# A six-layer cross network on one core: the second layer's weights on another DMA queue, and small loads moved to GpSimd's queue

## The chip, the cores and the metric

The kernel runs on one NeuronCore of a Trainium2 chip. The metric is the device time of one execution in microseconds (us), the median of several runs. Engine names in the profile: PE is TensorE (PEld its weight loads), DVE is VectorE, ACT is ScalarE, POOL is GpSimd, and SP is SyncE, which here only issues DMAs. "SPq" and "ACTq" are DMAs issued by SP and by ACT.

## The reference

```python
B, F, D, L = 4096, 26, 16, 6
Din = min(F * D, 1024)                 # 416
# x0: (4096, 416)   ws: (6, 416, 416)   bs: (6, 416), all bfloat16
def reference(x0, ws, bs):
    x = x0
    for l in range(ws.shape[0]):
        x = x0 * (x @ ws[l] + bs[l]) + x
    return x
```

Layer l needs all 416 features of layer l-1, so the six layers are strictly one after the other for each row; the 4096 rows are independent.

## The kernel before, in words

**Tiling.** The rows are cut into four blocks (`s`, 1024 rows), each into two halves (`h`, 512 rows). The data is kept with features on partitions: 416 = 3 x 128 main features (chunks `c`, `m` or `k`, `DF` = 384) and a tail of 32 (`DR`). The tail of the four quarters of a block sits on the four groups of 32 partitions. The kernel keeps sums in PSUM over the layers: layer l adds its product onto what is there, and VectorE makes the next input from it in one instruction per chunk and half, (PSUM + summed bias) x x0 (`leave`, line 429). ScalarE, GpSimd and two small copies do the same for the tail (`leave_tail` with `tail_halves`, line 439, the product in line 452, and `swap`, lines 416 and 418).

**One layer on TensorE**, in this order: `main` for half 0 (36 matmuls), `tail_rows` (the tail features as inputs; weights `wt_sb` and, for tail to tail, `wc_sb`), `tail_outs` (the tail as output, 12 matmuls over both halves), `main` for half 1 (36 matmuls). Nearly all matmuls are recorded under line 285, the helper `mm`.

**Weights.** `w_sb[:, l]` holds rows 0 to 383 of layer l ("W0" comes in three pieces, "W1" to "W5" each in one DMA of 312 KB by `load_main`). `wt_sb[:, l]` holds the 32 tail rows, four copies, one for each group of partitions ("wt0" is layer 0, "wt1" layer 1, "wt2" layers 2 to 5). `wc_sb` is zero but for the 32x32 corner of each layer (tail rows, tail columns), placed at four positions. In the kernel before, GpSimd zeroes `wc_sb` (line 272) and copies each corner out of `wt_sb` (`corner`, line 278): layer 0 ahead of the loop, layer 1 after the tail of layer 0, layers 2 to 5 after the tail of layer 1.

**Head.** The first 512 rows of x0 come in plainly (`xin_sb`, half by SP, half by ACT), are transposed on TensorE (line 500) and copied out of PSUM by VectorE and, for chunk 1, by ScalarE (lines 510 and 515). The other 512 rows of block 0 come by one transposing DMA (`load_transposed`, line 205) and their tail columns plainly (`xtl_sb`); `tail_in` brings the tail of block 0 into place through TensorE and one ScalarE copy (line 405) to `x0t_sb`. `bias_sums` needs the bias vectors in `bsa_sb[1:7]`, a row of ones and a small triangular matrix `u_sb`; ScalarE copies the sums to `cb_sb` (line 534).

**Order.** Every engine works through its instructions in the order in which they are added. `Plan.add` (line 28) derives the waits from the keys an operation reads and writes; operations on one engine do not wait for each other, except where a result is read (GpSimd's operations that shift data between partitions wait for the ones they depend on). DMAs of one queue are issued in program order. SP issues x0's first rows, W0, `xtl`, the transposing load, then W1, wt1, W2, wt2, W3 to W5, and the later blocks of x0; ACT issues x0's second rows, the bias vectors, wt0.

Of the kernel before, what the change touches and what calls it, by code (L numbers as in the profile page):

```python
# [15 lines left out]
class Plan:  # L16
# [11 lines left out]
    def add(self, eng, fn, reads=(), writes=(), adds=(), parts=(), dma=None, shifts=False):  # L28
        if eng == "gpsimd" and dma is None:
            if shifts:  # L30
                adds = tuple(adds) + (("shift",),)
            else:
                reads = tuple(reads) + (("shift",),)
        op = Op()
        op.eng, op.fn, op.marked, op.dma, op.waits = eng, fn, False, dma, []
        needs = []
        for key in tuple(reads) + tuple(adds):
            needs += [(w, True) for w in self.writer.get(key, ())]
            if key[0] == "ps":
                needs += [(r, False) for r in self.readers.get(key, ())]  # L40
        for key in tuple(writes) + tuple(adds):
            needs += [(w, True) for w in self.writer.get(key, ())]
            needs += [(r, False) for r in self.readers.get(key, ())]
        for key in parts:
            needs += [(r, False) for r in self.readers.get(key, ())]
        clock = self.clock[eng]
        for need, raw in sorted(needs, key=lambda n: -n[0].idx):
            lane = need.group if need.dma else need.eng
            if dma and need.dma == dma:
                continue  # L50
            if need.dma is None and need.eng == eng and dma is None and (eng == "tensor" or not raw):
                continue
            if clock.get(lane, -1) >= need.idx:
                continue
            op.waits.append(need)
            need.marked = True
            for lane2, idx in need.clock.items():
                clock[lane2] = max(clock.get(lane2, -1), idx)
            clock[lane] = max(clock.get(lane, -1), need.idx)
        op.idx = len(self.ops[eng])  # L60
        op.group = None
        if dma:
            op.group = ("dma", dma)
            members = self.groups.setdefault(op.group, [])
            members.append(op)
            op.marked = True
        op.clock = dict(clock)
        self.ops[eng].append(op)
        for key in reads:
            self.readers.setdefault(key, []).append(op)  # L70
        for key in parts:
            if self.readers.get(key):
                self.writer[key], self.readers[key] = [], []
            self.writer.setdefault(key, []).append(op)
        for key in tuple(writes) + tuple(adds):
            old = self.writer.get(key, ())
            keep = [w for w in old if dma and w.dma == dma]
            self.writer[key] = keep + [op]
            if not keep:
                self.readers[key] = []  # L80
        return op
# [37 lines left out]
def bass_standalone__dcn_v2_cross__recsys_kernel(  # L119
# [22 lines left out]
    with ExitStack() as es:  # L142
# [45 lines left out]
        def load(queue, dst, src, name, writes):  # L188
            P.add(queue, lambda e: e.dma_start(dst, src), writes=writes, dma=name)  # L189

        def load_main(l):
            load(
                "sync", w_sb[:, l, :, :], ws[l, 0:DF, :].rearrange("(k p) n -> p k n", p=128), "w%d" % l, [("w", l)]
            )

        def load_rows(queue, i):
# [33 lines left out]
        load_rows("scalar", 1)  # L230
        for k in CH:
            load("sync", w_sb[:, 0, k, :], ws[0, 128 * k:128 * k + 128, :], "w0_%d" % k, [("w", 0, k)])
        load("scalar", bsa_sb[1:L + 1, :], bs[:, :], "bs", [("bs",)])
        load(
            "scalar", wt_sb[:, 0, :], ws[0, DF:D, :].unsqueeze(0).to_broadcast([4, DR, D]), "wt0", [("wt", "wt0")]
        )
        load("sync", xtl_sb[:, 4:JS, :], x0_v[:, 4:JS, DF:D], "xtl0", [("xtl", 0)])
        load_transposed(0, H, SB)
        load_main(1)
        load_tail_weights(1, 2, "wt1")  # L240
        load_main(2)
        load_tail_weights(2, L, "wt2")
# [3 lines left out]
        for s in range(1, NS):  # L246
# [16 lines left out]
            ), reads=[("ones",)], writes=[("ident",)],  # L263
        )
        P.add("gpsimd", lambda e: e.memset(bsa_sb[0:1, :], 1.0), writes=[("bs1",)])
        P.add(
            "gpsimd", lambda e: e.affine_select(
                out=u_sb[:, :], in_=ones_sb[0:L + 1, 0:L], pattern=[[1, L]],
                compare_op=ALU.is_ge, fill=0.0, base=1, channel_multiplier=-1,
            ), reads=[("ones",)], writes=[("u",)],  # L270
        )
        P.add("gpsimd", lambda e: e.memset(wc_sb[:, :, :, :], 0.0), writes=[("wc", "wt%d" % i) for i in range(3)])

        def corner(a, b, name):
            for g in range(4):
                p = quad(g | 1)
                P.add(
                    "gpsimd", lambda e, p=p, g=g: e.tensor_copy(  # L278
                        out=wc_sb[p, a:b, g % 2, quad(g)], in_=wt_sb[p, a:b, DF:D]
                    ), reads=[("wt", name), ("wc", name)], writes=[("wc", name, g)], shifts=True,  # L280
                )


# [47 lines left out]
        def tail_rows(s, l, start):  # L331
            src, key = src_tail(s, l)
            keys = [("wt", wkey(l)), key, key + ("swapped",)]

            def rows(pe, q, h, m, begin):
                for part in range(2):
                    if q % 2 == 0:
                        if part:
                            break
                        dst, rhs = ps[:, bank(h, m), :], src[quad(q), :, :]  # L340
                    else:
                        dst, rhs = ps[:, bank(h, m), part * G:(part + 1) * G], src[quad(q), 1 - part, :]
                    ins = mm(
                        pe, dst, wt_sb[quad(q), l, m * 128:(m + 1) * 128], rhs, begin and part == 0, (32 * q, 0)
                    )
                return ins

            def first(pe):
                for q in range(4):
                    h, m = divmod(q, 2)  # L350
                    ins = rows(pe, q, h, m, l == 0 and h == 1)
                return ins

            def second(pe):
                for q in range(4):
                    h = q // 2
                    if q % 2 == 0:
                        ins = rows(pe, q, h, 2, l == 0 and h == 1)
                    else:
                        for part in range(2):  # L360
                            ins = mm(
                                pe, ps[:, T_BANK[h], 0:G], wc_sb[quad(q), l, part, :], src[quad(q), 1 - part, :],
                                start and part == 0, (32 * q, 0),
                            )
                return ins

            P.add("tensor", first, reads=keys, adds=[("ps", bank(h, m)) for h in HALVES for m in range(2)])
            P.add(
                "tensor", second, reads=keys + [("wc", wkey(l), g) for g in range(4)],
                adds=[("ps", bank(h, 2)) for h in HALVES] + [("ps", T_BANK[h]) for h in HALVES],  # L370
            )

# [121 lines left out]
        for i in range(2):  # L494
            for c in CH:
                b = HEAD_BANKS[i][c]

                def fn(pe, i=i, c=c, b=b):
                    for j in range(2):
                        ins = pe.transpose(  # L500
                            out=psT[:, b, j * 128:(j + 1) * 128],
                            in_=xin_sb[:, 2 * i + j, c * 128:(c + 1) * 128], identity=ident[:, :],
                        )
                    return ins

                P.add("tensor", fn, reads=[("xin", i), ("ident",)], adds=[("ps", b)])
                dst, src = x0T_sb[:, c, i * 256:(i + 1) * 256], psT[:, b, 0:256]
                if c == 1:
                    P.add(
                        "scalar", lambda e, d=dst, s=src: e.activation(out=d, in_=s, func=ACTF.Copy),  # L510
                        reads=[("ps", b)], writes=[("x0Tp", c, i)],
                    )
                else:
                    P.add(
                        "vector", lambda e, d=dst, s=src: e.tensor_copy(out=d, in_=s),  # L515
                        reads=[("ps", b)], writes=[("x0Tp", c, i)],
                    )
# [20 lines left out]
            )  # L538


        corner(0, 1, "wt0")
        for s in range(NS):
            for l in range(L):
                ending = s == NS - 1 and l == L - 2
# [22 lines left out]
                leave_tail(s, l, not ending)  # L567
                if l == 2 and 0 < s < NS - 1:
                    place_tail(s + 1)
                if s == 0 and l == 0:  # L570
                    corner(1, 2, "wt1")
                if s == 0 and l == 1:
                    corner(2, L, "wt2")
                if l == 1 and s > 0:
                    store_block(s - 1)
                if ending:
# [151 lines left out]
```

## Time and profile before

| what | us |
|---|---|
| median of 3 runs (129.32 to 129.96) | 129.5 |
| the profiled execution, its own time | 130.31 |
| span of that execution on the core | 128.7 |
| TensorE busy | 124.5 (97% of the span) |
| VectorE busy | 98.3 |
| ScalarE busy | 44.3 |
| GpSimd busy | 39.6 |

The span is the part of an execution that the profile covers; 1.6 us of the profiled execution lie outside it. The granted TensorE clock is 1.0 over the span. A line of the timeline has the start, the duration (from the first to the last of a group), the engine, the line of the kernel, the operation, the tiles, the count, and in brackets how long the engine sat idle before it and what ended that.

### The profile page before, as it was taken

To read this page: it belongs to the slowest core of one execution; us is meant where nothing else is said; L and a number is where in the kernel's file an instruction comes from. 1 tells how busy PE (TensorE), PEld (TensorE's weight loads), DVE (VectorE), ACT (ScalarE), POOL (GpSimd) and SP (SyncE) were. 2 spreads that over 40 slices of the span, in tenths; PEclk is the share of its full clock that TensorE was granted. 3 is DMA by queue.
4 is the path that set the end of the run, shared out by engine and by line. 5 is a ranking of instruction groups with operands and counts; after the bars stand their busy time and mean duration, and the time that the engine had idled before them with its cause. 6 is when DMAs were issued, how large, how long until landed. Compare 5 with 4: busy or idle time off the path is not lost.

```text
span 128.7 us, 5290 instructions
## 1 busy us (share of the span) xinstructions
PE 124.5 (97%) x2402; PEld 64.5 (50%) x2402; DVE 98.3 (76%) x150; ACT 44.3 (34%) x97; POOL 39.6 (31%) x88
## 2 busy tenths in 40 slices
PE   7998999999999999999999999999999999999991
PEld 5553545545545545545545545545455455455660
DVE  0319489698797797797797797797797797797973
ACT  1525233343313243252222252252222252253920
POOL 7024273142122243242221251341320341440550
PEclk9999999999999999999999999999999999999999
DMA  3987999019999994500009407200008906100017
GB/s 110 198 203 184 265 210 231 21 37 233 195 177 240 172 166 157 156 8 5 0 5 189 81 0 248 63 5 0 0 5 167 103 5 216 54 0 5 0 38 232
DMA packets 34998, 14.11 MB, mean 110 GB/s; under 512 B 25690, under 2 KB 34976, under 8 KB 34976
## 3 DMA queue, kind: packets, MB, share of 16 engines
q1 hardware_dynamic: 34272, 13.24, 49.3%
q10 hardware_dynamic: 704, 0.54, 1.3%
q8 instruction: 19, 0.31, 1.0%
q14 instruction: 3, 0.02, 0.2%
HBM read 3.87 MB, written 3.41 MB: 57 GB/s over the span
## 4 chain that ended last, share of the span: by engine, by line
PE 88%; SPq 4%; DMA 4%; DVE 0%; issue 0%
PE ps L285 88%; DMA w_sb<-in_ws_dram 4%; SPq L205 2%; SPq L189 2%; DVE o_sb L659 0%
## 5 line engine op out<-in xcount | busy, mean ns | idle before, releaser
L429 DVE SCALAR_TENSOR_TENSOR xT_sb<-ps,cb_sb,x0T_sb 128x512 bf16<-128x512 f32 x120 | 80.9, 743 | 20.3 <-PE ps L285 20.3
L285 PE MATMUL ps<-xT_sb,w_sb 128*32 128x512 bf16 (+1 forms) x1596 | 84.2, 364 | 0.6 <-DMA w_sb<-in_ws_dram 0.6
L285 PEld LDWEIGHTS ps<-xT_sb,w_sb 128*32 128x32 bf16 x1596 | 40.8, 97 | 38.1 <-issue 4.0
L439 ACT ACTIVATE t_sb<-ps,cb_sb 64x256 f32<-64x256 f32 x46 | 21.6, 469 | 57.7 <-PE ps L285 57.4
L452 POOL TENSOR_TENSOR xt_sb<-t_sb,x0t_sb 128x256 bf16<-128x256 f32 x20 | 13.4, 672 | 63.4 <-ACT t_sb L439 63.4
L416 ACT ACTIVATE xt_sb<-xt_sb 32x256 bf16<-32x256 bf16 x38 | 15.7, 414 | 15.4 <-POOL xt_sb L452 15.2
L285 PE MATMUL ps<-x0T_sb,w_sb 128*32 128x512 bf16 (+1 forms) x336 | 19.3, 373 | 0.0
L418 POOL COPY xt_sb<-xt_sb 32x256 bf16<-32x256 bf16 x38 | 14.9, 392 | 2.4
L429 DVE SCALAR_TENSOR_TENSOR xo_sb<-ps,cb_sb,x0T_sb 128x512 bf16<-128x512 f32 x18 | 12.1, 744 | 2.5 <-PE ps L285 2.5
L285 PEld LDWEIGHTS ps<-x0T_sb,w_sb 128*32 128x32 bf16 x336 | 8.4, 98 | 7.6 <-issue 0.8
L285 PE MATMUL ps<-xt_sb,wt_sb 32*128 32x512 bf16 (+1 forms) x152 | 11.7, 326 | 0.0
L285 PE MATMUL ps<-xt_sb,wc_sb 32*128 32x256 bf16 x76 | 7.4, 268 | 0.0
L285 PEld LDWEIGHTS ps<-xt_sb,wt_sb 32*128 32x128 bf16 x152 | 2.4, 91 | 8.3 <-DVE xT_sb L429 6.4
L452 POOL TENSOR_TENSOR xot_sb<-t_sb,x0t_sb 128x256 bf16<-128x256 f32 x3 | 2.0, 672 | 9.9 <-ACT t_sb L439 9.9
L285 PE MATMUL ps<-w_sb,xT_sb 128*32 128x416 bf16 (+1 forms) x60 | 5.1, 339 | 0.0
L278 POOL COPY wc_sb<-wt_sb 32x32 bf16<-32x32 bf16 (+1 forms) x12 | 2.8, 233 | 5.1 <-DMA wt_sb<-in_ws_dram 4.5
L659 DVE TENSOR_TENSOR o_sb<-ps,xr_sb 128x416 bf16<-128x416 f32 x6 | 3.4, 587 | 1.3 <-PE ps L285 1.0
L293 PE MATMUL ps<-const-bfloat16-1.0 128*128 128x256 bf16 x14 | 3.1, 415 | 0.8 <-PEq L713 0.8
L285 PEld LDWEIGHTS ps<-xt_sb,wc_sb 32*128 32x128 bf16 x76 | 3.8, 93 | 0.2
L515 DVE COPY x0T_sb<-ps 128x256 bf16<-128x256 bf16 x4 | 1.1, 292 | 3.5 <-PE ps L500 3.2
L461 ACT ACTIVATE sS_sb<-ps,cb_sb 128x512 bf16<-128x512 f32 x5 | 3.0, 692 | 0.0
L285 PEld LDWEIGHTS ps<-w_sb,xT_sb 128*32 128x32 bf16 (+1 forms) x60 | 2.3, 97 | 1.4 <-issue 0.2
(39 smaller groups left out, 28.8 us busy)
## 6 DMA issues: line engine op xcount, KB each, us to landing
out_dram<-o_sb SPq DMA_DIRECT2D x3, 832.0 KB, 4.2
w_sb<-in_ws_dram SPq DMA_DIRECT2D x5, 312.0 KB, 4.4
xr_sb<-in_x_dram SPq DMA_DIRECT2D x1, 832.0 KB, 6.3
wt_sb<-in_ws_dram SPq DMA_DIRECT2D x4, 104.0 KB, 2.9
out_dram<-o_sb SPq DMA_DIRECT2D x2, 208.0 KB, 2.2
w_sb<-in_ws_dram SPq DMA_DIRECT2D x3, 104.0 KB, 3.6
xin_sb<-in_x_dram SPq DMA_DIRECT2D x1, 208.0 KB, 3.0
xin_sb<-in_x_dram ACTq DMA_DIRECT2D x1, 208.0 KB, 3.3
```

Source lines behind the costliest of these rows:

```text
L189: P.add(queue, lambda e: e.dma_start(dst, src), writes=writes, dma=name)
L205: "sync", lambda e: e.dma_start_transpose(x0T_sb[:, :, s * SB + a:s * SB + b], x0[s * SB + a:s * SB + b, 0:DF]),
L278: "gpsimd", lambda e, p=p, g=g: e.tensor_copy(out=wc_sb[p, a:b, g % 2, quad(g)], in_=wt_sb[p, a:b, DF:D]), reads=[("wt", name), ("wc", nam ...
L285: return pe.matmul(dst, lhsT=lhsT, rhs=rhs, start=start, stop=True, skip_group_check=True, tile_position=pos,)
L293: ins = pe.matmul(ps[:, 7, 0:256], lhsT=const[:, 0:128], rhs=const, start=True, stop=True)
L416: fn = lambda e, d=dst, s=src: e.activation(out=d, in_=s, func=ACTF.Copy)
L418: fn = lambda e, d=dst, s=src: e.tensor_copy(out=d, in_=s)
L429: "vector", lambda e: e.scalar_tensor_tensor(out=dst, in0=ps[:, bank(h, c), :], scalar=cb_sb[:, c, l:l + 1], in1=x0T_sb[:, c, o:o + H], op ...
L439: "scalar", lambda e, p=p, h=h: e.activation(out=dst[p, :], in_=ps[p, T_BANK[h], 0:G], func=ACTF.Identity, bias=cb_sb[p, NC, l:l + 1]), re ...
L452: "gpsimd", lambda e: e.tensor_tensor(out=dst, in0=t, in1=x0t_sb[:, s, 0, :], op=ALU.mult),
L461: fn = lambda e: e.activation(out=o, in_=i, func=ACTF.Identity, bias=b)
L659: "vector", lambda e: e.tensor_tensor(out=o_sb[:, jj, :], in0=ps[:, b, 0:D], in1=xr_sb[:, j, :], op=ALU.mult), reads=[("ps", b), ("xr",)], ...
```

## The change

W1 is issued by ACT, right behind wt0, and no longer by SP behind the transposing load. The bias vectors are issued by GpSimd's queue and no longer by ACT. The zeroing of `wc_sb` goes from GpSimd to VectorE. The corners of layers 1 to 5 are brought in by four DMAs on GpSimd's queue straight from `ws` (each 32 partitions x 5 layers x 64 bytes), right behind the build of `u_sb`; only layer 0's corner is still copied by GpSimd from `wt_sb`. Of the two PSUM copies of chunk 1 in the head, the first goes from ScalarE to VectorE. A GpSimd operation that shifts data waits for earlier GpSimd operations that do not shift.

```diff
@@ Plan.add
         for key in tuple(writes) + tuple(adds):
             needs += [(w, True) for w in self.writer.get(key, ())]
-            needs += [(r, False) for r in self.readers.get(key, ())]
+            needs += [(r, key == ("shift",)) for r in self.readers.get(key, ())]
@@ loads
-        def load_main(l):
+        def load_main(l, queue="sync"):
             load(
-                "sync", w_sb[:, l, :, :], ...
+                queue, w_sb[:, l, :, :], ...
             )
...
-        load("scalar", bsa_sb[1:L + 1, :], bs[:, :], "bs", [("bs",)])
         load(
             "scalar", wt_sb[:, 0, :], ws[0, DF:D, :].unsqueeze(0).to_broadcast([4, DR, D]), "wt0", [("wt", "wt0")]
         )
+        load_main(1, "scalar")
         load("sync", xtl_sb[:, 4:JS, :], x0_v[:, 4:JS, DF:D], "xtl0", [("xtl", 0)])
         load_transposed(0, H, SB)
-        load_main(1)
         load_tail_weights(1, 2, "wt1")
         load_main(2)
@@ GpSimd's start
         P.add("gpsimd", lambda e: e.memset(bsa_sb[0:1, :], 1.0), writes=[("bs1",)])
+        P.add("gpsimd", lambda e: e.dma_start(bsa_sb[1:L + 1, :], bs[:, :]), writes=[("bs",)], dma="bs")
...
-        P.add("gpsimd", lambda e: e.memset(wc_sb[:, :, :, :], 0.0), writes=[("wc", "wt%d" % i) for i in range(3)])
-
-        def corner(a, b, name):
+        P.add("vector", lambda e: e.memset(wc_sb[:, :, :, :], 0.0), writes=[("wc",)])
+        for g in range(4):
+            P.add(
+                "gpsimd", lambda e, g=g: e.dma_start(
+                    wc_sb[quad(g | 1), 1:L, g % 2, quad(g)], ws[1:L, DF:D, DF:D].rearrange("l p n -> p l n")
+                ), reads=[("wc",)], writes=[("wc1",)], dma="wc",
+            )
+
+        def corner():
             for g in range(4):
                 p = quad(g | 1)
                 P.add(
-                    "gpsimd", lambda e, p=p, g=g: e.tensor_copy(
-                        out=wc_sb[p, a:b, g % 2, quad(g)], in_=wt_sb[p, a:b, DF:D]
-                    ), reads=[("wt", name), ("wc", name)], writes=[("wc", name, g)], shifts=True,
+                    "gpsimd", lambda e, p=p, g=g: e.tensor_copy(out=wc_sb[p, 0, g % 2, quad(g)], in_=wt_sb[p, 0, DF:D]),
+                    reads=[("wt", "wt0"), ("wc",)], writes=[("wc0", g)], shifts=True,
                 )
@@ tail_rows
-                "tensor", second, reads=keys + [("wc", wkey(l), g) for g in range(4)],
+                "tensor", second, reads=keys + ([("wc1",)] if l else [("wc0", g) for g in range(4)]),
@@ head copies
-                if c == 1:
+                if i and c == 1:
                     P.add("scalar", ...)
@@ main loop
-        corner(0, 1, "wt0")
+        corner()
...
-                if s == 0 and l == 0:
-                    corner(1, 2, "wt1")
-                if s == 0 and l == 1:
-                    corner(2, L, "wt2")
```

More of the change, by code (lines that the diff above doesn't have):

```diff
@@ L189, in load @@
             P.add(queue, lambda e: e.dma_start(dst, src), writes=writes, dma=name)
-        def load_main(l):
+        def load_main(l, queue="sync"):
             load(
-                "sync", w_sb[:, l, :, :], ws[l, 0:DF, :].rearrange("(k p) n -> p k n", p=128), "w%d" % l, [("w", l)]
+                queue, w_sb[:, l, :, :], ws[l, 0:DF, :].rearrange("(k p) n -> p k n", p=128), "w%d" % l, [("w", l)]
             )
```

## Prediction

> **What bounds the kernel now.** I read the chain of work that ended last first, since it says which engine carries the end and what stands in front of it.
>
> ```profile
> 3.49 3.18 SPq L205 DMA_TRANSPOSE x0T_sb<-in_x_dram  x1
> 6.66 0.05 issue
> 6.71 5.47 DMA w_sb<-in_ws_dram
> 12.18 0.04 issue
> 12.22 113.84 PE ps L285 x2160
> ```
>
> From 12.22 us on TensorE carries the end alone. What releases it there is W1: issued by SP at 6.71, behind a transposing load whose issue holds SP for 3.18 us, it lands 5.47 us later. So a microsecond won before 12.22 is worth a microsecond, and so is any later hole in TensorE's row. The timeline of the first 30 us shows the holes.
>
> ```profile
> 7.01 1.00 POOL L278 COPY wc_sb<-wt_sb 32x32 bf16<-32x32 bf16 x4 [3.76 <-DMA wt_sb<-in_ws_dram]
> 7.27 0.10 PEld L285 LDWEIGHTS ps<-ident,xin_sb 128*32 128x32 bf16 x2
> 8.58 0.12 PEld L285 LDWEIGHTS ps<-x0t_sb,wt_sb 32*128 32x128 bf16 x8 [0.55 <-ACT x0t_sb L405]
> 8.71 0.21 PEld L285 LDWEIGHTS ps<-x0t_sb,wc_sb 32*128 32x128 bf16 x4
> 12.22 2.13 PE L285 MATMUL ps<-xT_sb,w_sb 128*32 128x512 bf16 x36 [0.64 <-DMA w_sb<-in_ws_dram]
> 14.28 0.12 PEld L285 LDWEIGHTS ps<-xt_sb,wt_sb 32*128 32x128 bf16 x8 [0.42 <-issue]
> 18.14 1.34 POOL L278 COPY wc_sb<-wt_sb 32x128 bf16<-32x128 bf16 x4
> 19.16 0.76 PE L285 MATMUL ps<-xt_sb,wt_sb 32*128 32x512 bf16 x7
> 24.19 0.60 PE L285 MATMUL ps<-xt_sb,wt_sb 32*128 32x512 bf16 x7
> 29.07 0.60 PE L285 MATMUL ps<-xt_sb,wt_sb 32*128 32x512 bf16 x7
> ```
>
> The start of the tail matmuls marks each layer: 8.58, 14.28, 19.16, 24.19, 29.07. The last pitch, 4.88 us, is that of an undisturbed layer (14.28 to 19.16 is 4.88 too). From layer 0 to layer 1 it is 5.70, so W1 costs 0.82 us, of which 0.64 are recorded as idle. From layer 2 to layer 3 it is 5.03: GpSimd's copies of the corners of layers 2 to 5 run to 19.48, and TensorE waits for them, 0.15 us. That is all the change can win: 0.97 us, 0.75%.
>
> Then the DMA engines, since W1 is to move among the first loads; the columns are busy time (and count) by engine, granted clock, DMA share and GB/s.
>
> ```profile
> 2.00:3.00 1.00, 1.00 (x7) 0.67 (x5) 0.00 (x0) 0.34 (x1) 1.00 (x1) 1.00 0.92 265
> 3.00:4.00 1.00, 1.00 (x8) 0.55 (x7) 0.00 (x0) 0.99 (x2) 0.25 (x1) 1.00 1.21 330
> 4.00:5.00 1.00, 1.00 (x12) 1.00 (x10) 0.62 (x3) 0.55 (x2) 0.00 (x0) 1.00 0.57 145
> 6.00:7.00 1.00, 1.00 (x28) 0.30 (x24) 0.00 (x0) 0.03 (x1) 0.00 (x0) 1.00 0.53 91
> xtl_sb<-in_x_dram SPq DMA_DIRECT2D x1, 32.0 KB, 4.3
> ```
>
> They are full from 2 to 4 us and half free from 4 to 5 and from 6 to 7. The last line, from the list of issues, is the tightest load in the head: `xtl`, issued at 2.75, lands at 7.05, and `tail_in` needs it at 7.27 (second line of the block before). GpSimd has nothing to do from 3.26 to 7.01.
>
> **The change part by part.** The sum is made in the profiled execution, whose own time (130.31) is 0.81 above the median, its span (128.7) 0.8 below; the difference is applied to the median, 129.5.
>
> *W1 leaves SP.* ACT's issues become x0's rows (0.79 to 1.30), wt0 (0.64, the bias's slot at 1.33) and W1 (issue rows of `w_sb` 0.43 to 0.57), to about 2.6. That is where ACT's table load started before (2.66, 1.28 long), so ACT is not later. At the slowest landing shown for `w_sb` (5.5 us) W1 is there at 8.1, needed at 11.4 (12.22 - 0.82): minus 0.82. Next in line for layer 1 are VectorE's results of half 0 (three of 0.74 from 9.05, done at 11.1) and wt1, whose copies were done in time before; SP now issues wt1 and all behind it 0.6 earlier. Nothing takes the place of that wait.
>
> *Corners by DMA.* The copies at 13.09 and 18.14 go, the second with its 0.15. TensorE first needs the DMAs that replace them at about 13.6 (layer 1's tail, 14.42 - 0.82). At the price that I take below the last is issued by 6.5; with the slowest landing shown (5.5) it is there at 12.0, with the rows of like size (wt1, 26 KB, 2.5) at 9. At the dearest price (9.3) and the slowest landing it would be 1.2 late, less than what TensorE then has lost already (rival 2). Minus 0.15.
>
> *W1 among the first loads.* Its 312 KB take 0.97 us at 330 GB/s. Nothing of it is new traffic, but it is now ahead of, or beside, `xtl` and the transposing load. If it finds the free halves of 4 to 5 and 6 to 7, `xtl` is no later: 0. If it pushes `xtl` by its whole length, `tail_in` starts 0.97 - 0.22 = 0.75 late, and all of TensorE with it. wt0 is 0.66 us earlier on its queue, which W1 then uses; that speaks for the lower half. I take 0.30. The transposed half of x0 is issued at 3.49 and lands at most 5.1 later, 8.6; `tail_outs` needs it at 9.14, or 9.44 when `tail_in` is 0.3 late; cover 0.8 against 0.97 at worst: 0 to 0.15, taken as 0.
>
> A rule of the Trainium skill speaks against this part: "DMA: Bandwidth & Descriptors", Issuing engines are not separate DMA queues, says that DMAs issued by different engines end on the same 16 DMA engines, interleave, and that a second issuer saves only issue time. The trace agrees in so far as the DMA share is at 0.92 and 1.21 when both queues work. By the rule alone W1's 0.97 would fall wholly on its neighbours, and the sum would be 0.22 won rather than 0.67.
>
> *GpSimd's queue.* Five DMA issues stand ahead of `corner()`, which starts at 7.01 (wt0 landed) and ends at 8.01; `second` of `tail_rows` needs it at 8.71. GpSimd issued no DMA before, so the price is unknown. Cheapest row: 0.43 (plain issue on SP); dearest plain issue row: 1.46 (one of `wt_sb`). GpSimd is at 1.8 when the first is due, and `u_sb` is 0.18. At 0.43 it is free at 4.1; at 1.46 at 9.3, the corner is done at 10.3, and TensorE 1.6 late. The nearest rows of GpSimd itself, its two memsets (0.43 and 1.37, mean 0.9), lie around the middle; I take 0.9: free at 6.5, cost 0. It is free of cost up to 1.14 (1.14 x 5 + 2.0 = 7.7, corner at 8.7).
>
> The same page, SWDGE vs HWDGE vs iDMA, sends plain transfers to SP and ACT, because GpSimd builds descriptors in software; its table Latency and other measured facts gives about 1 us to the first byte. No run here shows it yet. By an estimate from that page, 1 us for each, GpSimd would be free at 7.0 and the sum the same.
>
> *Bias vectors.* Due at 6.62 (their matmuls). Issued at 1.8; with the landing rows of small loads (wt1: 2.2 to 4.3) they are there by 6.1: 0. At 5.5 they would be 0.7 late.
>
> *The rest.* The memset of `wc_sb` on VectorE (1.37 on GpSimd) has from 1.05 to 4.24, when VectorE's first copy starts: 0. The extra copy in VectorE's row: its copies of 0.29 started as close as 0.21 apart, so the copy that releases the first `main` slips by 0 to 0.3; the two before it left gaps of that size, so 0. The added wait makes layer 0's corner wait for `u_sb`, long done: 0.
>
> Sum: -0.82 - 0.15 + 0.30 = -0.67, so 128.8.
>
> **The rivals.**
> 1. *The gain is eaten at `tail_in`* (0.24). `xtl` takes W1's full 0.97, the transposed half some more, 640 small packets of the corners in between: 0.75 to 0.9 of the 0.97 are lost, 129.3 to 129.4. For it: engines full until 4 us, a slack of only 0.22. Against it: half-free engines from 4 to 5 and 6 to 7.
> 2. *GpSimd's issues hold up layer 0's corner: slower* (0.19). The point is 1.34 us for each issue (5 x 1.34, from 2.0 with `u_sb`, and 1.0 for the copies: 9.7, which is 8.71 + 0.97). At 1.46 the time is 129.5 - 0.97 + 1.6 = 130.1; at 1.8 the corner ends at 12.0 and the time is 131.8. For it: each corner DMA has 160 pieces of 64 bytes. Against it: all but one of the plain issues of weights and x0 are at 0.7 or less.
> 3. *W1 lands no earlier in effect* (0.05), stuck on its queue beyond 11.4: only the 0.15 are won, 129.35. Against it: no load took over 5.5.
>
> **How the numbers follow.** The forecast holds with 0.52; 0.5% of 129.5 is 0.65 us, about what a measurement can tell from no change. Its own range is 128.4 (0.97, and 0.1 for the scatter of the runs) to 129.0; 0.45 of it lies under 128.85, 0.07 above. Rivals 1 and 3 are within 0.5%, rival 2 counts as slower: 0.45, 0.36, 0.19. The range for 8 in 10 goes from 128.4 to 130.2, which leaves out the dear half of rival 2 and a little below.
>
> **What the profile after would show.** Right: the chain no longer has `w_sb` before TensorE's long piece; the second layer's tail starts 4.88 after the first's, the fourth's 4.88 after the third's; GpSimd's copies in line 278's place are four. Wrong: a weight load of `tail_in` or `tail_outs` that waits for `xtl_sb` or `x0T_sb` by more than 0.75 (rival 1), a wait for `wc_sb` in layer 0 (rival 2), for `bsa_sb` before the bias matmuls, or a later end of VectorE's head copies.

## The result, and the profile after

The changed kernel is slower: 130.88 us (median, 130.16 to 131.68) against 129.41 us of the kernel before in the same series (128.70 to 129.96), ratio 1.012 with a 95% interval of 1.0078 to 1.0161. A second series gave 130.28 against 129.13, ratio 1.0109 (1.0067 to 1.0151). So 1.2 to 1.5 us were lost where 0.7 were forecast as won. One run of the first series (131.68) had a granted clock of 0.987 and without it the median is 130.72; three of the kernels below had one run each at 0.987 or less that was over 1.5% longer than their fastest, and their medians leave it out.

The profiled execution of the changed kernel took 130.72 us with a span of 129.2. First its chain of the work that ended last (start, length, what):

```profile
2.76 5.33 DMA xtl_sb<-in_x_dram
8.09 0.14 issue
8.23 0.43 PE ps L290 x16
...
8.69 0.60 ACT x0t_sb L410
...
9.34 34.63 PE ps L290 x648
...
44.00 4.05 DVE xT_sb L434 x6
...
48.48 3.31 DMA ot_sb<-xot_sb
...
51.84 0.40 POOL o_sb L485
...
53.93 72.61 PE ps L290 x1388
```

`w_sb` no longer stands before TensorE's long piece, as was said. But two other things do. In the head the chain starts with `xtl_sb`: issued at 2.76 as before, it lands 5.33 us later, at 8.09, where it took 4.3 before; `tail_in` (8.23) and ScalarE's copy hang on it. And TensorE's long piece is cut at 44 to 54 us by a chain over a transposing DMA into `ot_sb` and GpSimd.

The same in the timeline of the changed kernel (start, length, engine, line, operation, tiles, count, idle time before and what ended it):

```profile
1.77 0.76 POOL L265 DMA_DIRECT2D bsa_sb<-in_bs_dram  x1
...
2.68 2.35 POOL L275 DMA_DIRECT2D wc_sb<-in_ws_dram  x4
...
6.29 1.00 POOL L284 COPY wc_sb<-wt_sb 32x32 bf16<-32x32 bf16 x4 [1.26 <-DMA wt_sb<-in_ws_dram]
...
8.23 0.23 PE L290 MATMUL ps<-ident,xin_sb 128*32 128x128 bf16 x2 [0.66 <-DMA xtl_sb<-in_x_dram]
...
9.33 0.12 PEld L290 LDWEIGHTS ps<-x0t_sb,wt_sb 32*128 32x128 bf16 x8 [0.54 <-ACT x0t_sb L410]
...
9.93 1.96 PEld L290 LDWEIGHTS ps<-x0T_sb,w_sb 128*32 128x32 bf16 x48 [0.26 <-DMA x0T_sb<-in_x_dram]
...
14.26 0.60 PE L290 MATMUL ps<-xt_sb,wt_sb 32*128 32x512 bf16 x7
...
19.14 0.60 PE L290 MATMUL ps<-xt_sb,wt_sb 32*128 32x512 bf16 x7
...
24.02 0.60 PE L290 MATMUL ps<-xt_sb,wt_sb 32*128 32x512 bf16 x7
...
48.41 0.60 PE L290 MATMUL ps<-xt_sb,wt_sb 32*128 32x512 bf16 x7
...
51.84 0.40 POOL L485 COPY o_sb<-ot_sb 128x256 bf16<-128x256 bf16 x1 [4.58 <-DMA ot_sb<-xot_sb]
...
53.93 0.59 PE L290 MATMUL ps<-xt_sb,wt_sb 32*128 32x512 bf16 x7 [0.57 <-POOL xt_sb L423]
```

The tails of the first four layers now start at 9.33, 14.26, 19.14 and 24.02. The pitch is the time from one such start to the next, 4.88 us where nothing disturbs a layer. Both pitches that were to shrink did: 5.70 became 4.93, and 5.03 became 4.88. At the last two rows of this kind, 48.41 and 53.93, the pitch is 5.5 (5.49 from weight load to weight load). But the first tail starts 0.75 later than the 8.58 of before, and the transposed half of x0 (9.93) now makes TensorE wait as well. GpSimd is done with its five DMA issues at 5.03 and waits for wt0 from then on.

Last, what the DMA engines do in these microseconds (stretch and its length; busy time and count on PE, PEld, DVE, ACT and POOL; granted clock; DMA share; GB/s):

```profile
4.00:5.00 1.00, 1.00 (x12) 1.00 (x10) 0.73 (x4) 0.40 (x2) 1.00 (x2) 1.00 0.76 189
5.00:6.00 1.00, 1.00 (x11) 0.33 (x13) 0.49 (x2) 0.38 (x1) 0.04 (x1) 1.00 1.08 307
6.00:7.00 1.00, 1.00 (x32) 0.31 (x28) 0.00 (x0) 0.11 (x1) 0.58 (x3) 1.00 1.52 242
7.00:8.00 1.00, 0.57 (x12) 0.08 (x4) 0.00 (x0) 0.08 (x1) 0.24 (x2) 1.00 1.09 216
```

The stretches from 4 to 5 and from 6 to 7, half free before (145 and 91 GB/s), carry 189 and 242 GB/s, and the one from 5 to 6 rose from 202 to 307. W1's parts land from 6.12 to 7.58, so its bytes did run in these stretches. TensorE stands still for 0.43 us of the stretch from 7 to 8.

### The profile page after: what moved, and what is told of

Read it like the earlier page. It is cut to its first block, busy times and chain, and to the rows that moved or that the text cites. A ratio compares the mean times of both kernels' runs of the same rounds, so it can differ in the third digit from the quotient of the medians.

```text
span 129.2 us, 5281 instructions
## 1 busy us (share of the span) xinstructions
PE 124.4 (96%) x2402; PEld 64.6 (50%) x2402; DVE 99.1 (77%) x152; ACT 43.9 (34%) x96; POOL 39.4 (30%) x84
## 4 chain that ended last, share of the span: by engine, by line
PE 83%; DMA 7%; DVE 4%; SPq 2%; POOL 1%; issue 1%; ACT 0%
PE ps L290 83%; DMA xtl_sb<-in_x_dram 4%; DVE xT_sb L434 3%; DMA ot_sb<-xot_sb 3%; SPq L189 1%; POOL xt_sb L423 1%; POOL xt_sb L457 1%; ACT x0t_sb L410 0%; DVE o_sb L660 0%; POOL o_sb L485 0%; SPq L474 0%
## 5 line engine op out<-in xcount | busy, mean ns | idle before, releaser
L671 POOL TENSOR_TENSOR o_sb<-f_sb,xr_sb 128x416 bf16<-128x416 f32 x2 | 1.9, 968 | 2.9 <-ACT f_sb L667 2.9
```

Source lines behind the costliest of these rows:

```text
L671: "gpsimd", lambda e: e.tensor_tensor(out=o_sb[:, jj, :], in0=t, in1=xr_sb[:, j, :], op=ALU.mult),
```

## The theories

Two facts asked for an explanation: the late head (+0.75 at the first tail), and that the 0.82 and 0.15 us won back from the two waits do not show in the time at all.

- *The transfers* (A in the expectations of all runs but the first). W1's 312 KB, now beside `xtl` and the transposing load on the same 16 DMA engines, make both late. Then W1's move alone must cost as much as the whole change, less of W1 must cost less, and `xtl` ahead of W1 must win back its part.
- *The accident* (B). The wait for W1 that the prediction removed belongs to the one execution that was profiled, not to the kernel. Then another profile of the kernel before must be without it.
- *The rival in GpSimd's part:* the five issues, or the corner DMAs' 640 small packets, do the harm. Then the change without W1's move must be slow.
- *The store* (C in the expectations): the hole at 51 to 54 us, where `store_block` puts a copy (line 485) that waits for a late DMA into GpSimd's queue ahead of the tail's product, is what costs the time; one layer later it should be gone.
- *Outside the span* (D): some of the loss lies outside what the profile covers, and goes with the DMAs that SP issues.
- *wt0's form* (E): wt0, one DMA with a source read four times over, lands in four parts (at 5.36 to 6.16 in the profile above), so it may keep a few engines busy longest and hold up what stands behind it; as four DMAs it should let `xtl` land in time.

## The experiments

### The kernel before, profiled once more

No edit.

> The kernel before, unchanged, profiled a second time. Theory A (the W1 wait of 0.82 us is a property of the kernel): the tail of layer 1 again starts 5.7 us after that of layer 0. Theory B (it was an accident of one execution, since 15 of W1's 16 parts had landed by 9.9 us and one at 12.18, behind an instruction fetch of 0.95 us on the same DMA engine): the pitch is below 5.3, because W1 lands by about 11.5, and the execution is about 0.5 to 0.9 us shorter than the first profiled one.

The execution took 129.66 us, span 128.4. Timeline:

```profile
8.70 0.60 PE L285 MATMUL ps<-x0t_sb,wt_sb 32*128 32x512 bf16 x7
...
13.58 0.60 PE L285 MATMUL ps<-xt_sb,wt_sb 32*128 32x512 bf16 x7
...
18.45 0.12 PEld L285 LDWEIGHTS ps<-xt_sb,wt_sb 32*128 32x128 bf16 x6 [0.42 <-POOL wc_sb L278]
...
53.15 0.59 PE L285 MATMUL ps<-xt_sb,wt_sb 32*128 32x512 bf16 x7 [0.32 <-POOL xt_sb L418]
```

From the first tail to the second it is 4.88 us, the pitch of an undisturbed layer. The wait for W1 is not there. By the record of landings in the trace the last part of W1 lands at 10.2, and it is needed at about 11.5. In the execution profiled first it was different: 15 of W1's 16 parts had landed by 9.9, the last at 12.2. The view of the DMA queues of that execution, from 9.5 to 12.3 us, has a row that suggests a reason (packets, MB, share of the engines):

```profile
q8 instruction: 1, 0.02, 2.1%
```

This is one fetch of instructions, 16 KB, that took 0.95 us from 9.83 on. It does not explain the late part by itself: a fetch of the same size and length ran in the second execution too, from 9.36 to 10.31, and W1's last part landed at 10.22 there. The trace does not tell on which of the 16 DMA engines a packet ran. So what made the one part late is open. What is shown is that the wait is not in every execution.

The times fit: the first execution's span less its 0.82, 128.7 - 0.82 = 127.9, is the median span of the 67 runs of the kernel before in the three later series (127.2 to 129.1), and its own time, 130.31, is reached by only 2 of them. The profile of the changed kernel with W1 back on SP and the store late, further down, has no wait for W1 either (tails at 8.33 and 13.21). The wait at layer 2 (0.15, by the copies of line 278) is in both profiles of the kernel before. In the second there is also a hole at 53 us (0.32, a pitch of 5.24), which is therefore not the change's doing alone.

### W1's move alone

The kernel before, with this one edit (the argument `queue` as in the change):

```diff
+        load_main(1, "scalar")
         load("sync", xtl_sb[:, 4:JS, :], x0_v[:, 4:JS, DF:D], "xtl0", [("xtl", 0)])
         load_transposed(0, H, SB)
-        load_main(1)
```

> The kernel before with one part of the change alone: W1 on the ACT queue behind wt0 (bias vectors still on ACT, corners still copied by GpSimd, memset and head copies as before). Theory A (W1 among the first loads makes xtl late): xtl lands at about 8 us instead of 7.05, tail_in starts 0.7 to 1.0 late, the time is 0.4 to 1.4 us above before. Rival (the small packets of GpSimd's queue make it late): xtl stays within 0.3 us of 7.05, tail_in is on time, W1's wait is gone, the time is at or up to 0.8 us below before.

130.31 us, ratio to before 1.0093 (1.0058 to 1.0129): the loss of the whole change within the intervals. Timeline:

```profile
8.08 0.23 PE L285 MATMUL ps<-ident,xin_sb 128*32 128x128 bf16 x2 [0.66 <-DMA xtl_sb<-in_x_dram]
...
9.19 0.12 PEld L285 LDWEIGHTS ps<-x0t_sb,wt_sb 32*128 32x128 bf16 x8 [0.55 <-ACT x0t_sb L405]
...
14.06 0.12 PEld L285 LDWEIGHTS ps<-xt_sb,wt_sb 32*128 32x128 bf16 x8 [0.42 <-issue]
```

`xtl` lands at 8.04, and TensorE waits for it as in the full change. The loss has two parts: the median span is 128.8, 0.9 over before's 127.9, and the median outside the span is 1.5 where it was 1.25, another 0.25; together 1.15. (The profiled execution, 129.96 with a span of 128.4, is the shortest of the six.)

### The rest of the change alone

The changed kernel, W1 back on SP behind the transposing load:

```diff
-        load_main(1, "scalar")
         load("sync", xtl_sb[:, 4:JS, :], x0_v[:, 4:JS, DF:D], "xtl0", [("xtl", 0)])
         load_transposed(0, H, SB)
+        load_main(1)
```

> The changed kernel with W1 put back on SP behind the transposing load; bias vectors and corners stay on GpSimd's queue. Theory A: xtl lands within 0.3 us of 7.05, tail_in is on time, the wait for the corners at layer 2 is gone, the time is that of before or 0.15 us below. Rival (GpSimd's packets): xtl is late by 0.5 or more and the time is 0.5 to 1.5 us above before.

128.97 us, ratio 0.9998 (0.9968 to 1.0027), over 11 runs. GpSimd's issues, the corner DMAs, the bias vectors and the two operations that went to VectorE, without W1's move, cost nothing that can be measured. Whether they win the 0.15 of layer 2 the interval, 0.4 us to either side, cannot tell. With the run before, W1's move is enough for the whole loss, and the rival in GpSimd's part falls as its cause. That GpSimd's part does no harm next to W1 does not follow from this (see "All together").

### A third of W1

W1's move alone, but only its first 104 KB on ACT's queue; the other 208 KB stay on SP behind the transposing load:

```diff
-        load_main(1, "scalar")
+        load("scalar", w_sb[:, 1, 0, :], ws[1, 0:128, :], "w1", [("w", 1)])
         load("sync", xtl_sb[:, 4:JS, :], x0_v[:, 4:JS, DF:D], "xtl0", [("xtl", 0)])
         load_transposed(0, H, SB)
+        load("sync", w_sb[:, 1, 1:3, :], ws[1, 128:DF, :].rearrange("(k p) n -> p k n", p=128), "w1", [("w", 1)])
```

> As the run with W1 alone on the ACT queue, but with a third of W1 (104 KB) there and two thirds on SP in the old place. Theory A, a dose: xtl is late by a third of the 0.9 us, so it lands at 7.3 to 7.45, hardly after its need of 7.27; the time is within 0.4 us of before. Rival (it is the second queue being busy at all, not its bytes): xtl lands at 7.8 or later and the time is that of the whole W1 on ACT, about 1.1 us above before.

129.39 us, ratio 1.0018 (0.9984 to 1.0051). Timeline:

```profile
8.59 0.12 PEld L286 LDWEIGHTS ps<-x0t_sb,wt_sb 32*128 32x128 bf16 x8 [0.55 <-ACT x0t_sb L406]
...
13.47 0.14 PEld L286 LDWEIGHTS ps<-xt_sb,wt_sb 32*128 32x128 bf16 x8 [0.42 <-issue]
```

`xtl` lands at 7.01, and the head is that of the kernel before. A third of the delay was expected (7.3 to 7.45), so the delay does not grow in proportion to the bytes. ACT's queue holds as many DMAs as in the run with all of W1, so it is the bytes ahead of `xtl` and the transposed half that cost, not one more DMA on ACT. W1 is still in time, and no gain shows.

### `xtl` first

W1's move alone, and `xtl` issued by SP ahead of W0:

```diff
+        load("sync", xtl_sb[:, 4:JS, :], x0_v[:, 4:JS, DF:D], "xtl0", [("xtl", 0)])
         for k in CH:
             load("sync", w_sb[:, 0, k, :], ws[0, 128 * k:128 * k + 128, :], "w0_%d" % k, [("w", 0, k)])
...
         load_main(1, "scalar")
-        load("sync", xtl_sb[:, 4:JS, :], x0_v[:, 4:JS, DF:D], "xtl0", [("xtl", 0)])
         load_transposed(0, H, SB)
```

> W1 on the ACT queue as in the run with that part alone, and xtl issued by SP ahead of the three pieces of W0 instead of behind them. Theory A (W1 pushes xtl and the transposing load back on the shared DMA engines): tail_in no longer waits for xtl, the next wait is for the transposed half of x0, which lands at about 9.2 to 9.6 and is needed at 9.1 to 9.3; layer 0's tail starts by 8.8 and the time is 0.3 to 0.7 us under that run's 130.31. Rival (W1 slows TensorE's start in some other way, not by xtl): layer 0's tail stays at 9.1 or later and the time stays within 0.2 us.

129.78 us, ratio 1.0048 (1.0017 to 1.0078): half the loss is back, and half stays. Timeline:

```profile
8.88 0.12 PEld L285 LDWEIGHTS ps<-x0t_sb,wt_sb 32*128 32x128 bf16 x8 [0.42 <-ACT x0t_sb L405]
...
9.57 1.96 PEld L285 LDWEIGHTS ps<-x0T_sb,w_sb 128*32 128x32 bf16 x48 [0.34 <-DMA x0T_sb<-in_x_dram]
```

`xtl` is there at 4.35. What TensorE waits for now is the transposed half, which lands at 9.53 where it landed at 8.55 and 8.65 in the two profiles of before. The last piece of W0, now issued behind W1, lands at 8.08 instead of 6.25 and costs a short wait too (0.35, ahead of the matmuls at 8.13). So W1's bytes fall on whichever load stands behind them.

### The store one layer later

The changed kernel, and then the changed kernel without W1's move, each with:

```diff
-                if l == 1 and s > 0:
+                if l == 2 and s > 0:
                     store_block(s - 1)
```

> The changed kernel with the copy and the store of the previous block's output moved from layer 1 to layer 2 of the next block, so that GpSimd doesn't stand in that copy while the tail product waits. Theory C (about 0.6 us of the loss is GpSimd held by the late transposes of block 0's output, shown in the profile after as a pitch of 5.49 in block 1): that pitch falls to 4.88 and the time is 0.4 to 0.8 us below that of the changed kernel (130.88), so 130.1 to 130.5. Rival (that hole is an accident of the profiled execution): no difference beyond 0.3 us.

130.33 us, ratio 1.0076 (1.004 to 1.0112). Timeline, block 1:

```profile
51.56 0.84 POOL L423 COPY xt_sb<-xt_sb 32x256 bf16<-32x256 bf16 x2
...
52.47 0.40 POOL L485 COPY o_sb<-ot_sb 128x256 bf16<-128x256 bf16 x1
...
53.56 0.60 PE L290 MATMUL ps<-xt_sb,wt_sb 32*128 32x512 bf16 x7
```

GpSimd's copies of the tail now run ahead of the store's copy, and TensorE does not wait; the pitch there is 4.88, where it was 5.49. The hole is gone, but the time is not clearly better than the 130.28 and 130.88 of the change.

> The changed kernel with W1 back on SP and with the copy and store of the previous block's output one layer later. Theory C (the runs of before differ among themselves mostly by GpSimd waiting for the transposes of block 0's output, up to 0.6 us): the time is 0.2 to 0.5 us under that with W1 back on SP alone, so 128.5 to 128.8, with less scatter, and faster than both kernels. Rival: within 0.15 us of it.

129.19 us, ratio 1.0002 (0.9975 to 1.003); all pitches of the first layers are 4.88 in its profile. It is not faster than the same without the late store (0.9998). So the hole is real in single executions (a pitch of 5.24 in one profile of before and none in the other, 5.49 in two of the change, 5.57 with a third of W1 moved, 5.08 with one more DMA on SP, none with W1's move alone, with `xtl` first or with wt0 in four), but what taking it away is worth is below what these runs can tell. As an account of the loss it falls.

### One more DMA on SP

W1's move alone, and a load of SP that is needed only much later (x0's rows for the end, `xr_sb`) split in two:

```diff
-        load("sync", xr_sb[:, :, :], x0_v[:, (NS - 1) * JS:NJ, :], "xr", [("xr",)])
+        for a in (0, 4):
+            load("sync", xr_sb[:, a:a + 4, :], x0_v[:, (NS - 1) * JS + a:(NS - 1) * JS + a + 4, :], "xr", [("xr",)])
```

> As the run with W1 alone on the ACT queue, with the last block's late load of x0 split in two DMAs on SP, so that SP has as many DMAs as in the kernel before. In all kernels with W1 off SP the time outside the span was 1.5 us, in those with W1 on SP mostly 1.25. Theory D (that goes by the length of SP's program): outside the span 1.25, the time 0.25 under 130.31. Rival (it goes with W1's place): outside the span still 1.5, no difference.

130.06 us, ratio 1.0065 (1.0034 to 1.0096). In 9 of 10 runs 1.23 to 1.30 us lie outside the span, where all six runs of W1's move alone had 1.48 to 1.56; the median span is hardly another, 128.7 against 128.8. So 0.25 us of the loss went with what SP has to issue and not with the head's transfers, which are as late here as before (`xtl` lands at 8.56). Why is open. Nor is the count the whole of it: the change without W1's move and with the late store, with as many DMAs on SP as before, had 1.24 to 1.29 in five of its runs and 1.56 to 1.77 in seven, and the one without the late store 1.75 to 1.81 in three of eleven.

### The change again, and wt0 in four DMAs

> The changed kernel once more, for a second profile and beside the next two on one chip. Theory A: xtl again lands at 7.8 or later and the transposed half of x0 at 9.2 or later, layer 0's tail starts at 9.2 or later; time 130.4 to 131.2. Rival (the profile after was as unlucky as the first one of before): xtl lands near 7.3 in this execution and layer 0's tail starts before 8.9.

This is the second series given at the top: 130.28 us. In its profiled execution `xtl` landed at 8.87 and the first tail started at 10.11. That execution took 131.41, 1.1 more than each of the other three (130.21 to 130.29), so its head is not the typical one of this kernel.

The change with wt0 split (and both PSUM copies of chunk 1 on VectorE, since ACT is then busy issuing):

```diff
-        load(
-            "scalar", wt_sb[:, 0, :], ws[0, DF:D, :].unsqueeze(0).to_broadcast([4, DR, D]), "wt0", [("wt", "wt0")]
-        )
+        for q in range(4):
+            load("scalar", wt_sb[quad(q), 0, :], ws[0, DF:D, :], "wt0", [("wt", "wt0")])
         load_main(1, "scalar")
...
-                if i and c == 1:
+                if False:
```

> The changed kernel with wt0 loaded by four DMAs of 32 partitions each, on ACT ahead of W1, instead of one DMA with a fourfold source (and with all head copies on VectorE, since ACT is busy issuing). The one DMA lands in four parts, so it runs on four DMA engines, and the traces show xtl and the transposing load waiting for the slowest. Theory E (those four engines, each with a fourth of wt0 and then its part of W1, are what makes xtl late): xtl lands by 7.2, the transposed half by 8.8, layer 0's tail starts at 8.3 to 8.8, the span is 127.5 to 127.9 and the time 129.0 to 129.4. Rival (it is W1's bytes on all engines alike): xtl still lands at 7.6 or later and the time stays above 130.2.

130.39 us, ratio 1.0099 (1.0068 to 1.013): nothing is won. Timeline:

```profile
8.56 0.13 PEld L289 LDWEIGHTS ps<-x0t_sb,wt_sb 32*128 32x128 bf16 x8 [0.55 <-ACT x0t_sb L409]
...
10.18 2.45 PE L289 MATMUL ps<-x0T_sb,w_sb 128*32 128x256 bf16 x48 [0.99 <-DMA x0T_sb<-in_x_dram]
```

`xtl` is nearly in time again (7.32) and the first tail starts at 8.56, but this does not show that wt0's form was the reason: ACT, with four issues for wt0, issues W1 only at 3.29 instead of 2.49, behind `xtl` (2.77). The transposed half lands at 10.14, and the wait is now in front of `tail_outs`. As a cure this falls: the load that waits has changed, and the second tail starts at 14.51, between the 14.26 and 14.98 of the change itself.

The same with the late store and the split `xr_sb` of the last two sections:

> As the run before it, and the copy and store of the previous block's output one layer later, and the late load of x0's last block split in two on SP. If theory E holds, span 127.3 to 127.7, 1.25 outside it, time 128.6 to 128.9: 0.2 to 0.4% under the kernel before. If it doesn't, 129.9 or more.

130.01 us, ratio 1.0067 (1.0043 to 1.0091), with 1.20 to 1.30 us outside the span. The first tail starts at 8.23, the second at 14.47. No kernel that was run beats the one before; the two without W1's move equal it.

### All together

Times are medians of each kernel's own series. Landings and starts are those of the one profiled execution of each kernel; "transposed" is the transposed half of x0. What the head lost shows in the start of the second tail.

| kernel | us | ratio to before | `xtl` lands | transposed lands | tail 0 starts | tail 1 starts |
|---|---|---|---|---|---|---|
| before, first profile | 130.31 (that execution) | | 7.05 | 8.55 | 8.58 | 14.28 (W1 late) |
| before, second profile | 129.14 | | 7.17 | 8.65 | 8.70 | 13.57 |
| change without W1's move, late store | 129.19 | 1.0002 | 6.85 | 8.72 | 8.33 | 13.21 |
| a third of W1 moved | 129.39 | 1.0018 | 7.01 | 8.50 | 8.59 | 13.47 |
| W1 moved, `xtl` first | 129.78 | 1.0048 | 4.35 | 9.53 | 8.88 | 13.89 |
| W1 moved, one more DMA on SP | 130.06 | 1.0065 | 8.56 | 9.80 | 9.71 | 14.59 |
| W1 moved | 130.31 | 1.0093 | 8.04 | 9.32 | 9.19 | 14.06 |
| change, wt0 in four, late store, one more DMA on SP | 130.01 | 1.0067 | 6.99 | 10.10 | 8.23 | 14.47 |
| change, late store | 130.33 | 1.0076 | 8.16 | 10.17 | 9.40 | 14.54 |
| change, wt0 in four | 130.39 | 1.0099 | 7.32 | 10.14 | 8.56 | 14.51 |
| change, first series | 130.88 | 1.012 | 8.09 | 9.89 | 9.33 | 14.26 |
| change, second series (profile of a run of 131.41) | 130.28 | 1.0109 | 8.87 | 10.58 | 10.11 | 14.98 |

With all of W1 moved the transposed half lands at 9.3 to 10.6, without it or with a third of it at 8.5 to 8.7, in every profile. `tail_outs` started at 9.13 and 9.25 in the two profiles of before.

The packets in the traces show more of how the loads wait for each other. The transposed half comes in 1536 packets of 256 bytes. In eleven of the twelve traces (not in that of wt0 in four) 9 to 22 of these that have started stand still for over 0.4 us, and nearly all of them end within 0.1 us of one another: at 6.90 and 7.00 in the two profiles of before, at 6.85 with a third of W1 moved, at 7.74 with all of it, at 7.31 and 8.04 in the change. The late parts of `xtl` land just behind that instant: 11 of 16 at 6.96 to 7.05 in the first profile of before (the other five by 5.73), 13 of 16 at 7.85 to 8.04 with W1 moved (the other three by 6.35). So, by these times, `xtl` does not lose a share of the bandwidth bit by bit: its last parts and the transposed half come behind one and the same instant, and with all of W1 ahead that instant comes later. What these packets wait for no run shows.

And the transposed half lands 1.6 to 1.7 us after that instant in all six traces without the corner DMAs and 2.4 to 2.7 after it in the five with them. Without W1's move that does not show, since there the instant comes at 6.33 and the transposed half is still there at 8.72. Next to W1 the transposed half then lands at 9.9 or later. A kernel with W1 moved and the rest of the change without the corner DMAs was not run, nor wt0 in four without them, so which part of the GpSimd change does this is open.

## Why the prediction was wrong

**"W1 leaves SP: minus 0.82" is the step that failed.** The mechanism was read rightly: in the profiled execution W1 held TensorE up by 0.82, and after the change it is there at 7.6 (8.1 was reckoned). But the typical execution holds no such wait. The prediction saw that the profiled execution was 0.81 us above the median and took it for a general offset between that execution and the others ("the difference is applied to the median"). Its span stands 0.8 above the median span of the later series (128.7 against 127.9), and that is the wait's 0.82. (Another 0.35 of its time lay outside the span: 1.6 where 1.25 is usual. Against the later medians, 129.13 to 129.16, it stood out by 1.15 to 1.18; that 0.81 fits the wait so closely owes something to the median of three runs.) What was removed had already been absent from the time it was subtracted from. The table of times showed it: 130.31 lies above all three runs (129.32 to 129.96), and a wait found in one execution, on a load landing 5.5 us after its issue where the median of the loads of that kind is 4.4, was a reason for doubt.

**"W1 among the first loads: plus 0.30" was the right mechanism, mis-sized.** 0.30 at `tail_in` meant `xtl` 0.52 later, since it had a slack of 0.22. It was later by 0.9 in the first profile (8.09 against 7.17) and by 1.7 in the second, and the first tail by 0.6 (9.33 against 8.70) and 1.4. Even the upper bound, 0.75, was too small for the second, which was, however, a run 1.1 us longer than its series. The bound took W1's bytes at the best rate seen (330 GB/s) and let them delay `xtl` alone. The hope that W1 would find the half-free stretches from 4 to 5 and 6 to 7 us came true, and did not help: the late parts of `xtl` landed behind one instant that came later with W1 ahead, and a mean share of the engines does not show that.

Here the prediction weighed a rule of the Trainium skill, "DMA: Bandwidth & Descriptors", Issuing engines are not separate DMA queues: DMAs of different issuers interleave on the same 16 engines, and a second issuer saves issue time only. The runs side with it in that the second issuer won nothing: with 312 KB of W1 on ACT `xtl` lands at 8.04 and the time is 0.9% longer. With 104 KB, however, it lands at 7.01, no later than before, so the bytes did not fall on the neighbours in full.

**"The transposed half: 0 to 0.15, taken as 0" was too small as well.** It lands at 9.3 to 10.6. In the change it hides behind the late `xtl` for the greater part; with `xtl` first a wait of 0.34 for it stays, beside the 0.35 for W0's last piece, and with wt0 split it is the wait in the head (0.99).

**Right, by its steps:** the corners by DMA took the wait at layer 2 away (5.03 to 4.88, minus 0.15). GpSimd's issues cost no time on the path; 0.9 us each was taken, and they took 0.76 for the bias vectors and 0.57 to 0.64 for each corner DMA, so GpSimd is free at 5.0 instead of 6.5. The bias vectors (there at 6.4, due at 6.6), VectorE's memset (0.70 long) and its extra copy show no wait of TensorE behind them. All of this together gives the 0.9998 of the run without W1's move; the 0.15 is within its interval. What the part on GpSimd's queue left out is what its DMAs may do to the transposed half: 2.4 to 2.7 instead of 1.6 to 1.7 behind the common instant.

**The rivals.** Rival 1 had what happened in its place, `tail_in` behind `xtl`, with a price (0.75 to 0.9) near what the head lost in the first profile (0.6 to 0.75). It came out as "no change" only because it stood against the 0.97 that were to be won, of which 0.82 were not there. Rival 2 had the sign for a cause that did not occur: its point was 1.34 us for each issue. Rival 3 did not occur. Two rows that were quoted hold for the head alone: over the whole kernel the dearest plain issue is that of `xr_sb`, 1.50, not 1.46, and loads take up to 6.3 (`xr_sb`) and 6.5 (transposing, the median), not 5.5. Nothing in the sum hangs on them.

**The sum, with the terms as measured,** between the two profiled executions of before (second, 129.66) and after (130.72): start of the second tail +0.69 (14.26 - 13.57), layer 2 -0.15, the hole at 53 us +0.25 (pitch 5.49 against 5.24), outside the span +0.26 (1.52 against 1.26). That is +1.05; the two differ by 1.06. The removed wait for W1 is no term of it, as the second profile of before has none. The hole's term is not part of what the change does in the median, as far as the runs tell.

## What to carry to other kernels

A wait is worth its length only if the typical execution has it: compare the profiled execution's own time with the other runs, and if it stands out by about the wait's length or more, profile the kernel again before anything is priced. A load that is issued earlier is paid for by the loads that it overtakes, so list the slack of each of these (here 0.2 and 0.6 us) against the moved bytes before the wait that is to go; here a third of the bytes could be moved at no cost that shows, and all of them could not. And check whether the loads that are overtaken wait for something in common, as the last parts of two loads did here. Whoever cures one late load in a full stretch should say which load is late next: here there always was one.

## What the runs showed of the hardware

- In one execution the last of 16 parts of a load landed 2.3 us behind the other 15 (12.18 against 9.89), and TensorE waited 0.82; in the next execution of the same kernel it landed 0.2 behind (10.22 against 10.01). Fetches of instructions, 16 KB and 0.95 us each at this point, ran on the DMA engines in both. With a granted clock of 0.998 or more the span of this one program varied from 127.2 to 129.1 us over 67 runs.
- The time outside the span is not a constant of the kernel: mostly 1.25 us with W1 on SP, 1.5 with it on ACT, 1.25 again with another DMA put on SP instead. The cause is open.
- A DMA issue on GpSimd took 0.76 us for the 6 bias rows and 0.57 to 0.64 for 160 pieces of 64 bytes: as cheap as SP's plain issues (0.43 to 0.69), and here on an engine that had the time.
- Packets of a transposing load that had started were let go on all sides within 0.1 us of one another, 6.90 in one profile of the kernel before and 7.74 with W1 moved, and most parts of the 32 KB load issued ahead of it landed only behind that instant (6.96 to 7.05 and 7.85 to 8.04). What they wait for is open.
- In the whole change `xtl` landed at 8.09 and 8.87 with wt0 as one DMA whose source is read four times, and at 7.32 and 6.99 with wt0 as four DMAs. In the latter W1 was issued 0.8 us later, behind `xtl`, so these landings do not tell what wt0's form does; no run changed it alone.
